# A pseudo-inverse formed in a thread of its own, and a shorter hold of the second batch

## The chip, the cores and the metric

The kernel runs on one core of one Trainium2 chip. The metric is the device time of one execution in microseconds (us), as a median of runs; profiles come from a single profiled execution.

## The reference

Landmark attention (32 landmarks) over 8 batches, 8 heads, 576 tokens and 64 columns a head, then a Fourier mix of the result and an MLP, with weights w1 (512 x 2048) and w2 (2048 x 512). Cut to what matters:

```python
# q_lm, k_lm: means of 18 tokens each, 32 landmarks
A = sm(q, k_lm); Bm = sm(q_lm, k_lm); C = sm(q_lm, k)      # row softmax of scaled products
Z = Bm.T / (norm1(Bm) * norminf(Bm) + 1e-06)
for _ in range(6):
    Z = 2 * Z - Z @ Bm @ Z
out = A @ Z @ C @ v
u = x + real(fft(fft(x, axis=1), axis=2))                  # x: the heads of out side by side
un = (u - mean) / sqrt(var + 1e-06)
result = u + relu(un @ w_ch1) @ w_ch2
```

## The kernel before

The kernel writes one long program for the five engines. `Kernel.run` is a planner: it holds generators ("threads") with priorities, and lets the first one that is due write instructions, until that one yields a time to wait. The planner's clock `self.now` is its own estimate of TensorE's time; `till(...)` is the estimated wait until tiles are ready, and `banks=` adds the wait for a free PSUM bank. The order of TensorE's instructions is exactly the order in which the threads write them, and TensorE runs them in that order: an instruction that waits holds back all behind it. The order on the other engines is arranged by the scheduler of the language.

The threads are: `attention` (priority 1), which runs `tokens` for one batch after the other; `landmarks` of a batch (priority 0), spawned from `tokens`; `weights` (priority 2), which decodes w1 and w2 from 64-bit words and splits each into a high and a low half of 16 bits, 32 pieces in all; and `mlp` (priority 3). The MLP works on chunks of 256 tokens (two tiles). For each of eight pairs of hidden blocks it forms a first product (24 matmuls `h<-unT,w`) and a second product (12 matmuls `acc<-w,h`), which trails two pairs behind. `self.seconds` counts the second products written so far. In chunk 0 the first four hidden tiles lie in buffers of the pool "mid" (seven), the others in the pool "h" (four).

Attention of a batch is two parts that meet in `mix`:
- `tokens`: sums of the landmarks (`lm`), splits of q, the products A (`at<-kbd,big`), their softmax, transposes, and the Fourier sums along the tokens (`CS`).
- `landmarks`: the product B of the landmarks and its row softmax `nrm`; C (`at<-big,qbd`, four PSUM banks) with its exponentials `Ces`; the norm product `psn` (`at<-nrm,ones_bd`), which gives the scale `ci` (and `nci`, its negative) of the inverse; the block-diagonal form `Bbd` of B, its transpose `BT`, and E = I - ci * BT'BT; the transposes `ETs` of `Ces` and their product with v, which gives R. Then comes an iteration of six steps: E is squared, and R is multiplied by I + E at each step. Both stand side by side in the tile `RE` (32 columns of E, 64 of R), so one step is `at<-RE,E` with 96 columns for each of two groups of four heads. Last, `at<-RE,Bbd` and `at<-Bbd,RE` give the small matrix from which `Wx`, `Wt` and the tables `WC` for `mix` come.

Batch 1 starts when w1 is split. In both its parts stands a hold, before C and before A:

```python
while b == 1 and self.seconds < NF // 2 - HB:   # NF // 2 - HB = 4
    yield 0.5
```

All f32 matmuls appear as two instructions each in the profile, f32 transposes as one. In the profile's names, `at` is a PSUM tile of the attention, `big`, `mid` and `row` are buffers, `h` a hidden tile, `acc` the sum of second products, `u` the normalised rows' input, `unT` its transpose by DMA. In `at<-RE,E` the tile E is stationary and RE moves.

Of the kernel before, what the change touches and what calls it, by code (L numbers as in the profile page):

```python
# [10 lines left out]
F32 = mybir.dt.float32  # L11
# [3 lines left out]
ALU = mybir.AluOpType  # L15
AX = mybir.AxisListType

P = 128
H, S, D, LM, DM, DF = 8, 576, 64, 32, 512, 2048
NF = DF // P  # L20
# [6 lines left out]
BIG, MID, ROW, UB, HB, NT, PSH = 8, 7, 6, 7, 4, 3, 2  # L27
# [6 lines left out]
MARGIN, NM, AM, M0 = 1.5, 2.0, 2.0, 0.2  # L34
# [91 lines left out]
class Kernel:  # L126
# [67 lines left out]
    def mm(self, out, a, b, start=True, stop=True, share=1.0):  # L194
        self.there[out.name] = self.now
        self.now += share * (0.42e-3 if a.dtype == F16 else 1.0e-3) * math.prod(b.shape[1:])
        self.nc.tensor.matmul(out, a, b, start=start, stop=stop, skip_group_check=True)  # L197

    def tr(self, out, a, ident):
        self.there[out.name] = self.now  # L200
        self.now += 0.11
        self.nc.tensor.transpose(out, a, ident)  # L202
# [155 lines left out]
    def tokens(self, b, st):  # L358

        nc, mm, mm3, tr, sm, split = self.nc, self.mm, self.mm3, self.tr, self.sm, self.split  # L360
        V, A = self.V, self.A
# [27 lines left out]
        e, r = yield from self.pow2(am, 4, "ab")  # L389
# [15 lines left out]
        for g in range(2):  # L405
# [5 lines left out]
                )  # L411
            if g == 0:
                yield self.till(qhs[0], kbd)
        while b == 1 and self.seconds < NF // 2 - HB:
            yield 0.5

        scr = self.small(1, "scr")
# [3 lines left out]
        for u in range(3):  # L421
            yield self.till(qhs[min(u, 1)])
            ps = self.psum()
            nh, scA = (16, sc[:, 4 + u : 5 + u]) if u < 2 else (4, scr)
            for j in range(4) if u < 2 else range(2):
                rows, at, g = (slice(0, P), 128 * j, u) if u < 2 else (slice(64 * j, 64 * j + 64), 0, j)
# [6 lines left out]
            pv, av = (t[:, 0:w].rearrange("p (h m) -> p h m", m=32) for t in (ps, ae))  # L433
# [11 lines left out]
        for u in range(3):  # L445
            ae, w = aes[u], 512 if u < 2 else 128
            AT = (self.mid() if u < 2 else self.row()).bitcast(F16)[:, 0 : 2 * w].rearrange("p (y t) -> p y t", y=2)
            if b < 2:
                yield self.till(ae, banks=1)
                ps = self.psum()  # L450
# [31 lines left out]
        for x in range(2):  # L482
            yield self.till(*Fs, banks=2)
            pss = [self.psum(), self.psum()]
            for g in range(2):
                for o in range(2):
                    i = (3, 0)[o] if x == 0 else (1, 2)[o]
# [12 lines left out]
        st["CS"] = CS  # L500
        st["tokens"] = [*st["AT"], CS]

    def landmarks(self, b, st):

        nc, mm, tr, sm = self.nc, self.mm, self.tr, self.sm
        V, A = self.V, self.A
        loads, qbd, lm = st["loads"], st["qbd"], st["lm"]
        m4g = lambda m: self.mask4.unsqueeze(1).unsqueeze(3).broadcast_to([P, 2, 4, m])
        wide = lambda src, m: src.unsqueeze(2).broadcast_to([P, 2, 4, m])
        Bd = sm.tile([P, 2, 32], F32, name="Bd")  # L510
        RE = sm.tile([P, 2, 96], F32, name="RE", bufs=3)
        Ces, crs = [], []


        ps = self.psum()
# [12 lines left out]
        nrm = sm.tile([P, 2, 2, 32], F32, name="nrm", bufs=1)  # L528
# [5 lines left out]
            rs.unsqueeze(2).broadcast_to([P, 2, 32]), ALU.mult,  # L534
        )

        while b == 1 and self.seconds < NF // 2 - HB:
            yield 0.5

        for g in range(2):  # L540
# [4 lines left out]
            for hf in range(2):  # L545
                ps = self.psum()
# [15 lines left out]
            V.reciprocal(cr, cr)  # L562
            Ces.append(Ce)
            crs.append(cr)
        yield self.till(nrm)

        psn = self.psum()
        mm(psn[:, 0:128], self.ones_bd.rearrange("p a b -> p (a b)"), nrm.rearrange("p g x m -> p (g x m)"))
        cm = self.small(4, "cm")
        V.tensor_reduce(cm, psn[:, 0:128].rearrange("p (x m) -> p x m", m=32), AX.X, ALU.max)  # L570
        ci = self.small(2, "ci")
        cmv = cm.rearrange("p (g x) -> p g x", x=2)
        V.tensor_tensor(ci, cmv[:, :, 0], cmv[:, :, 1], ALU.mult)
        V.tensor_scalar(ci, ci, 1e-6, None, ALU.add)
        V.reciprocal(ci, ci)
        nci = self.small(2, "nci")
        V.tensor_scalar(nci, ci, -1.0, None, ALU.mult)
        Bbd = sm.tile([P, 2, 4, 32], F32, name="Bbd", bufs=1)
        V.tensor_tensor(Bbd, wide(nrm[:, :, 0, :], 32), m4g(32), ALU.mult)
        yield self.till(Bbd, Ces[0])  # L580
        pst = self.psum()
        for g in range(2):
            tr(pst[:, 128 * g : 128 * g + 128], Bbd[:, g].rearrange("p a b -> p (a b)"), self.ident)
        BT = sm.tile([P, 2, P], F32, name="BT", bufs=1)
        A.copy(BT.rearrange("p g m -> p (g m)"), pst[:, 0:256])
        ETs = []
        for g in range(2):
            ET = self.mid().rearrange("p (t m) -> p t m", t=5)
            ps = self.psum()
            for t in range(4):  # L590
                tr(ps[:, 128 * t : 128 * t + 128], Ces[g][:, 128 * t : 128 * t + 128], self.ident)
            A.copy(ET[:, 0:4].rearrange("p t m -> p (t m)"), ps)
            ps = self.psum()
            tr(ps[:64, 0:128], Ces[g][:, 512:576], self.ident)
            A.copy(ET[:64, 4], ps[:64, 0:128])
            ETs.append(ET)
            if g == 0:
                yield self.till(BT, Ces[1])
                pse = self.psum()
                for i in range(2):  # L600
                    mm(pse[:, 128 * i : 128 * i + 128], BT[:, i], BT[:, i])
                E = sm.tile([P, 2, 4, 32], F32, name="E")
                for i in range(2):
                    V.scalar_tensor_tensor(
                        E[:, i].rearrange("p a b -> p (a b)"), pse[:, 128 * i : 128 * i + 128], nci[:, i : i + 1],
                        self.ident, ALU.mult, ALU.add,
                    )
                V.tensor_reduce(RE[:, :, 0:32], E.rearrange("p g a b -> p g b a"), AX.X, ALU.add)
        for g in range(2):
            yield self.till(ETs[g], loads[g][2])  # L610
            vf = loads[g][2].rearrange("p (c d) -> p c d", c=5)
            ps = self.psum()
            for t in range(5):
                n = P if t < 4 else 64
                for i in range(4):
                    mm(ps[32 * i : 32 * i + 32, 0:64], ETs[g][:n, t, 32 * i : 32 * i + 32], vf[:n, t, 64 * i : 64 * i + 64], t == 0, t == 4)
            V.tensor_scalar(RE[:, g, 32:96], ps[:, 0:64], crs[g], ci[:, g : g + 1], ALU.mult, ALU.mult)
        yield self.till(E, RE)


        for it in range(6):
            c0 = 0 if it < 5 else 32
            ps = self.psum()
            for g in range(2):
                mm(ps[:, 96 * g + c0 : 96 * g + 96], E[:, g].rearrange("p a b -> p (a b)"), RE[:, g, c0:])
            pv = ps[:, 0:192].rearrange("p (g m) -> p g m", g=2)
            nRE = sm.tile([P, 2, 96], F32, name="RE", bufs=3)
            if it < 5:
                E = sm.tile([P, 2, 4, 32], F32, name="E")
                V.tensor_tensor(E, wide(pv[:, :, 0:32], 32), m4g(32), ALU.mult)  # L630
                A.copy(nRE[:, :, 0:32], pv[:, :, 0:32])
            V.tensor_tensor(nRE[:, :, 32:96], RE[:, :, 32:96], pv[:, :, 32:96], ALU.add)
            RE = nRE
            yield self.till(E, RE, more=NM)

        ps, pst = self.psum(), self.psum()
        for g in range(2):
            mm(ps[:, 64 * g : 64 * g + 64], Bbd[:, g].rearrange("p a b -> p (a b)"), RE[:, g, 32:])
            for o in range(2):
                mm(pst[64 * o : 64 * o + 64, 64 * g : 64 * g + 64].rearrange("p (r m) -> p r m", r=2), RE[:, g, 32:], Bbd[:, g, o::2])  # L640
        wm = self.small(1, "wm")
        V.tensor_reduce(wm, ps[:, 0:128], AX.X, ALU.max, apply_absolute_value=True)
        yield self.till(wm)
# [12 lines left out]
        for i, at in enumerate((0, 32, 160, 128)):  # L656
# [3 lines left out]
            pv = ps[rows, 0:128].rearrange("p (g m o) -> p g m o", g=2, o=2)  # L660
# [5 lines left out]
        for g in range(2):  # L666
            for x in range(2):
                ps = self.psum()
# [292 lines left out]
```

## Time and profile before

| what | value |
|---|---|
| median of 3 runs | 1067.77 us (1065.95 to 1068.18) |
| the profiled execution | 1067.68 us |
| its span, first to last instruction | 1065.9 us |
| TensorE (PE) busy | 981.1 us, 92% |
| weight loads (PEld) | 681.0 us, 64% |
| VectorE (DVE) busy | 614.0 us, 58% |
| ScalarE (ACT) busy | 351.7 us, 33% |
| GpSimd (POOL) busy | 126.6 us, 12% |
| mean granted TensorE clock | 0.96 |

The page divides the span into 40 slices of 26.6 us; a digit is the busy share of a slice in tenths. A row of the table of stages gives, after the stretch, the busy time of each engine with its number of instructions in brackets, then the granted TensorE clock (1.00 is full), the DMA share and the rate. A row in order of time gives the start, the duration, the engine, the line, the operation, the output and inputs, the shape, the number of instructions merged, and in brackets how long the engine was idle before it and what ended that. A row of a group gives the number, then busy time and mean duration in ns, then the idle time before.

### The profile page before, as it was taken

Reading aid. Unit: us, or ns where it says so; the run is one execution under the profiler, and the core shown is the slowest. Engines: PE = TensorE matmul, PEld = TensorE weight load, DVE = VectorE, ACT = ScalarE, POOL = GpSimd, SP = SyncE. Lnnn points to the kernel's source line nnn. Section 1 sums busy time; section 2 is a strip of 40 time slices with the busy share of each in tenths; the row PEclk is TensorE's granted clock in tenths of the full one; section 3 lists DMA queues with packets and bytes.
Section 4 is the critical chain, followed back from the end, with each engine's and each line's share of the span. In section 5 each row is a group of like instructions: output and inputs, shape, how many; then the busy total and the mean of one; then the engine's idle time right before and its main releaser. Section 6 shows DMA issues by size and latency. Waiting matters only on the chain.

```text
span 1065.9 us, 19548 instructions
## 1 busy us (share of the span) xinstructions
PE 981.1 (92%) x8008; PEld 681.0 (64%) x8008; DVE 614.0 (58%) x1655; ACT 351.7 (33%) x791; POOL 126.6 (12%) x137
## 2 busy tenths in 40 slices
PE   1553779999999999999999999999999999999998
PEld 0442645677776677766776777667766677766665
DVE  7889888768553476446746574567451654341111
ACT  4566755324221333124322332243312332111110
POOL 0101101021101030110302030104010030110000
PEclk8556989999999999999999999999999999999999
DMA  9824402221401022111502050114111010120000
GB/s 328 311 83 129 141 25 91 70 42 39 152 21 35 26 80 103 21 31 21 179 4 50 11 164 19 40 21 129 64 41 21 21 23 20 21 50 16 5 21 20
DMA packets 85994, 71.70 MB, mean 67 GB/s; under 512 B 56336, under 2 KB 74768, under 8 KB 85776
## 3 DMA queue, kind: packets, MB, share of 16 engines
q1 hardware_dynamic: 85904, 70.45, 22.1%
q8 instruction: 63, 1.03, 0.4%
q14 instruction: 27, 0.22, 0.1%
HBM read 48.02 MB, written 9.44 MB: 54 GB/s over the span
## 4 chain that ended last, share of the span: by engine, by line
PE 86%; DVE 8%; issue 2%; ACT 2%; DMA 1%; POOL 0%; SPq 0%; ACTq 0%; DVEq 0%
PE acc L197 34%; PE h L197 34%; PE at L197 16%; DVE w L121 2%; DVE row L121 2%; DVE mid L121 1%; PE at L202 1%; ACT row L121 1%; DVE lm L121 1%; DMA big<-q_dram 0%; ACT mid L121 0%; DVE asum L121 0%; DVE u L121 0%; DVE RE L121 0%; POOL row L121 0%
## 5 line engine op out<-in xcount | busy, mean ns | idle before, releaser
L197 PE MATMUL h<-unT,w 128*128 128x256 f16 x3456 | 413.5, 274 | 20.3 <-DMA unT<-row 11.5
L197 PEld LDWEIGHTS <-w 128*128 128x128 f16 x3456 | 336.2, 98 | 92.8 <-issue 19.5
L197 PE MATMUL acc<-w,h 128*128 128x512 f16 x1680 | 394.8, 379 | 0.0
L197 PEld LDWEIGHTS <-h 128*128 128x128 f16 x1680 | 161.9, 98 | 160.5 <-issue 3.4
L121 DVE SCALAR_TENSOR_TENSOR h<-h 128x512 f16<-128x512 f32 x140 | 96.5, 689 | 247.5 <-ACT h L121 247.0
L121 ACT ACTIVATE h<-h 128x512 f16<-128x512 f32 x140 | 83.4, 596 | 367.9 <-PE h L197 367.5
L121 POOL TENSOR_TENSOR r<-ve,mhalf 128x2 f32<-128x2 f32 (+1 forms) x20 | 13.7, 683 | 446.7 <-DVE ve L121 446.7
L121 POOL TENSOR_TENSOR row<-row 128x512 f16<-128x512 f32 (+1 forms) x44 | 47.3, 1089 | 44.0 <-ACT row L121 44.0
L197 PEld LDWEIGHTS <-mid 128*128 128x128 f16 x432 | 40.2, 103 | 17.7 <-issue 9.0
L197 PEld LDWEIGHTS <-big 128*128 128x128 f16 (+1 forms) x768 | 41.3, 106 | 13.6 <-issue 2.4
L121 POOL TENSOR_TENSOR mid<-mid,asum 128x512 f32<-128x512 f32 x14 | 15.1, 1080 | 272.2 <-issue 134.5
L121 DVE TENSOR_REDUCE lm<-big 128x32 f32<-128x576 f32 (+1 forms) x48 | 44.2, 945 | 3.3 <-DMA big<-k_dram 3.2
L121 DVE SCALAR_TENSOR_TENSOR row<-at,scw,row 128x262 f32<-128x262 f32 (+1 forms) x48 | 21.4, 486 | 41.4 <-ACT row L121 27.2
L121 ACT CAST row<-row 128x512 f16<-128x512 f32 (+1 forms) x44 | 23.2, 557 | 64.5 <-DVE row L121 63.9
L121 ACT ACTIVATE row<-w 128x512 f32<-128x512 f32 x54 | 33.8, 641 | 22.8 <-DVE w L121 12.4
L197 PE MATMUL at<-RE,E 128*128 128x96 f32 (+1 forms) x192 | 31.1, 288 | 9.0 <-DVE RE L121 9.0
L121 DVE SCALAR_TENSOR_TENSOR u<-at,scw,row 128x128 f32<-128x128 f32 (+3 forms) x120 | 38.9, 389 | 0.0
L121 POOL TENSOR_TENSOR mid<-mid 128x256 f32<-128x256 f32 (+1 forms) x32 | 31.5, 987 | 61.5 <-DVE mid L121 54.0
L197 PEld LDWEIGHTS at<-RE,E 128*128 128x128 f32 x192 | 28.6, 205 | 15.3 <-issue 6.2
L121 DVE TENSOR_TENSOR mid<-mid 128x256 f32<-128x256 f32 x48 | 34.5, 743 | 1.6 <-POOL mid L121 1.4
L197 PE MATMUL at<-mid,big 128*128 128x262 f16 (+1 forms) x288 | 34.3, 293 | 0.0
L121 DVE SCALAR_TENSOR_TENSOR u<-acc,wsc,u 128x512 f32<-128x512 f32 x36 | 26.7, 745 | 11.5 <-PE acc L197 11.3
(167 smaller groups left out, 955.6 us busy)
## 6 DMA issues: line engine op xcount, KB each, us to landing
w<-w_dram SPq DMA_DIRECT2D x22, 512.0 KB, 8.9
big<-v_dram SPq DMA_DIRECT2D x16, 640.0 KB, 9.2
big<-q_dram SPq DMA_DIRECT2D x16, 584.0 KB, 5.2
big<-k_dram SPq DMA_DIRECT2D x16, 576.0 KB, 4.2
out_dram<-u SPq DMA_DIRECT2D x36, 256.0 KB, 2.0
big<-w_dram SPq DMA_DIRECT2D x10, 512.0 KB, 8.2
unT<-row SPq DMA_TRANSPOSE x72, 2.4
t<-t_dram SPq DMA_DIRECT2D x1, 1048.0 KB, 9.2
```

The costliest lines, as they stand in the source:

```text
L121: return call(out, *args, **kw)
L197: self.nc.tensor.matmul(out, a, b, start=start, stop=stop, skip_group_check=True)
L202: self.nc.tensor.transpose(out, a, ident)
```

## The change

`landmarks` now forms `psn`, `ci` and `nci` right after `nrm`, ahead of the hold and of C, and then spawns a new thread, `inverse`, with priority 0. That thread makes `Bbd`, `BT` and E, and runs the six steps without R: it carries E and the growing product of the (I + E) in a tile `EP` (32 columns each). The first step moves 32 columns, the next four 64, the last 32. Then it spreads the product to block-diagonal form (`Pbd`), multiplies it with `Bbd` and copies the result to G. `landmarks` goes on to C, the transposes and R (now a tile of its own), waits until G is there, and forms the last products from G and R. Both holds of batch 1 end after one second product, where they ended after four.

```diff
-        while b == 1 and self.seconds < NF // 2 - HB:
+        while b == 1 and self.seconds < 1:
             yield 0.5
...
+    def inverse(self, st, nrm, nci):
...
+        V.tensor_tensor(Bbd, wide(nrm[:, :, 0, :]), m4, ALU.mult)
+        yield self.till(Bbd, banks=1)
...
+            tr(ps[:, 128 * g : 128 * g + 128], flat(Bbd, g), self.ident)
...
+        A.copy(BT.rearrange("p g m -> p (g m)"), ps[:, 0:256])
+        yield self.till(BT, nci, banks=1)
...
+            mm(ps[:, 128 * g : 128 * g + 128], BT[:, g], BT[:, g])
...
+        V.tensor_reduce(EP[:, :, 0:32], E.rearrange("p g a b -> p g b a"), AX.X, ALU.add)
+        for it in range(6):
+            yield self.till(E, EP, banks=1, more=NM)
+            c0, c1 = (0 if it < 5 else 32), (64 if it > 0 else 32)
+            ps = self.psum()
+            for g in range(2):
+                mm(ps[:, 64 * g + c0 : 64 * g + c1], flat(E, g), EP[:, g, c0:c1])
...
+            if it < 5:
+                nE = sm.tile([P, 2, 4, 32], F32, name="E")
+                V.tensor_tensor(nE, wide(pv[:, :, 0:32]), m4, ALU.mult)
+                A.copy(nEP[:, :, 0:32], pv[:, :, 0:32])
+            if it == 0:
+                V.tensor_tensor(nEP[:, :, 32:64], EP[:, :, 0:32], self.diag32.unsqueeze(1).broadcast_to([P, 2, 32]), ALU.add)
+            else:
+                V.tensor_tensor(nEP[:, :, 32:64], EP[:, :, 32:64], pv[:, :, 32:64], ALU.add)
+            E, EP = nE, nEP
+        yield self.till(EP, banks=1)
+        Pbd = sm.tile([P, 2, 4, 32], F32, name="E")
+        V.tensor_tensor(Pbd, wide(EP[:, :, 32:64]), m4, ALU.mult)
+        yield self.till(Pbd, banks=1)
...
+            mm(ps[:, 128 * g : 128 * g + 128], flat(Pbd, g), flat(Bbd, g))
...
+        A.copy(G.rearrange("p g a b -> p (g a b)"), ps[:, 0:256])
+        st["G"] = G
...
     def landmarks(self, b, st):
...
+        yield self.till(nrm)
+        psn = self.psum()
+        mm(psn[:, 0:128], self.ones_bd.rearrange("p a b -> p (a b)"), nrm.rearrange("p g x m -> p (g x m)"))
...
+        self.spawn(self.inverse(st, nrm, nci))
+
+        while b == 1 and self.seconds < 1:
             yield 0.5
...
-        yield self.till(nrm)
-        psn = self.psum()
...
-            V.tensor_scalar(RE[:, g, 32:96], ps[:, 0:64], crs[g], ci[:, g : g + 1], ALU.mult, ALU.mult)
-        yield self.till(E, RE)
-        for it in range(6):
-            c0 = 0 if it < 5 else 32
...
+            V.tensor_scalar(R[:, g], ps[:, 0:64], crs[g], ci[:, g : g + 1], ALU.mult, ALU.mult)
+
+        while "G" not in st:
+            yield 0.3
+        Gt = st["G"]
+        yield self.till(Gt, R, banks=2)
...
-            mm(ps[:, 64 * g : 64 * g + 64], Bbd[:, g].rearrange("p a b -> p (a b)"), RE[:, g, 32:])
+            mm(ps[:, 64 * g : 64 * g + 64], Gt[:, g].rearrange("p a b -> p (a b)"), R[:, g])
             for o in range(2):
-                mm(pst[...], RE[:, g, 32:], Bbd[:, g, o::2])
+                mm(pst[...], R[:, g], Gt[:, g, o::2])
```

More of the change, by code (lines that the diff above doesn't have):

```diff
@@ L501, in tokens @@
         st["tokens"] = [*st["AT"], CS]
+    def inverse(self, st, nrm, nci):
+        mm, tr, sm, V, A = self.mm, self.tr, self.sm, self.V, self.A
+        m4 = self.mask4.unsqueeze(1).unsqueeze(3).broadcast_to([P, 2, 4, 32])
+        wide = lambda t: t.unsqueeze(2).broadcast_to([P, 2, 4, 32])
+        flat = lambda t, g: t[:, g].rearrange("p a b -> p (a b)")
+        Bbd = sm.tile([P, 2, 4, 32], F32, name="Bbd", bufs=1)
+        V.tensor_tensor(Bbd, wide(nrm[:, :, 0, :]), m4, ALU.mult)
[3 more added lines that the diff above has]
+            tr(ps[:, 128 * g : 128 * g + 128], flat(Bbd, g), self.ident)
+        BT = sm.tile([P, 2, P], F32, name="BT", bufs=1)
+        A.copy(BT.rearrange("p g m -> p (g m)"), ps[:, 0:256])
+        yield self.till(BT, nci, banks=1)
+        ps = self.psum()
+        for g in range(2):
+            mm(ps[:, 128 * g : 128 * g + 128], BT[:, g], BT[:, g])
+        E = sm.tile([P, 2, 4, 32], F32, name="E")
+        for g in range(2):
+            V.scalar_tensor_tensor(flat(E, g), ps[:, 128 * g : 128 * g + 128], nci[:, g : g + 1], self.ident, ALU.mult, ALU.add)
+        EP = sm.tile([P, 2, 64], F32, name="EP", bufs=3)
+        V.tensor_reduce(EP[:, :, 0:32], E.rearrange("p g a b -> p g b a"), AX.X, ALU.add)
+        for it in range(6):
+            yield self.till(E, EP, banks=1, more=NM)
+            c0, c1 = (0 if it < 5 else 32), (64 if it > 0 else 32)
+            ps = self.psum()
+            for g in range(2):
+                mm(ps[:, 64 * g + c0 : 64 * g + c1], flat(E, g), EP[:, g, c0:c1])
+            pv = ps[:, 0:128].rearrange("p (g m) -> p g m", g=2)
+            nEP = sm.tile([P, 2, 64], F32, name="EP", bufs=3)
+            if it < 5:
[11 more added lines that the diff above has]
+        yield self.till(Pbd, banks=1)
+        ps = self.psum()
+        for g in range(2):
+            mm(ps[:, 128 * g : 128 * g + 128], flat(Pbd, g), flat(Bbd, g))
+        G = sm.tile([P, 2, 4, 32], F32, name="G", bufs=1)
+        A.copy(G.rearrange("p g a b -> p (g a b)"), ps[:, 0:256])
+        st["G"] = G
@@ L507, in landmarks @@
         loads, qbd, lm = st["loads"], st["qbd"], st["lm"]
-        m4g = lambda m: self.mask4.unsqueeze(1).unsqueeze(3).broadcast_to([P, 2, 4, m])
-        wide = lambda src, m: src.unsqueeze(2).broadcast_to([P, 2, 4, m])
         Bd = sm.tile([P, 2, 32], F32, name="Bd")
-        RE = sm.tile([P, 2, 96], F32, name="RE", bufs=3)
+        R = sm.tile([P, 2, 64], F32, name="R", bufs=1)
         Ces, crs = [], []
@@ L535, in landmarks @@
         )
-        while b == 1 and self.seconds < NF // 2 - HB:
+        yield self.till(nrm)
+        psn = self.psum()
+        mm(psn[:, 0:128], self.ones_bd.rearrange("p a b -> p (a b)"), nrm.rearrange("p g x m -> p (g x m)"))
+        cm = self.small(4, "cm")
+        V.tensor_reduce(cm, psn[:, 0:128].rearrange("p (x m) -> p x m", m=32), AX.X, ALU.max)
+        ci = self.small(2, "ci")
+        cmv = cm.rearrange("p (g x) -> p g x", x=2)
+        V.tensor_tensor(ci, cmv[:, :, 0], cmv[:, :, 1], ALU.mult)
+        V.tensor_scalar(ci, ci, 1e-6, None, ALU.add)
+        V.reciprocal(ci, ci)
+        nci = self.small(2, "nci")
+        V.tensor_scalar(nci, ci, -1.0, None, ALU.mult)
+        self.spawn(self.inverse(st, nrm, nci))
+        while b == 1 and self.seconds < 1:
             yield 0.5
@@ L564, in landmarks @@
             crs.append(cr)
-        yield self.till(nrm)
-        psn = self.psum()
[L568 to L585, printed above, removed]
+        yield self.till(Ces[0])
         ETs = []
@@ L596, in landmarks @@
             ETs.append(ET)
[L597 to L608, printed above, removed]
         for g in range(2):
@@ L616, in landmarks @@
                     mm(ps[32 * i : 32 * i + 32, 0:64], ETs[g][:n, t, 32 * i : 32 * i + 32], vf[:n, t, 64 * i : 64 * i + 64], t == 0, t == 4)
-            V.tensor_scalar(RE[:, g, 32:96], ps[:, 0:64], crs[g], ci[:, g : g + 1], ALU.mult, ALU.mult)
-        yield self.till(E, RE)
-        for it in range(6):
-            c0 = 0 if it < 5 else 32
[L623 to L634, printed above, removed]
+            V.tensor_scalar(R[:, g], ps[:, 0:64], crs[g], ci[:, g : g + 1], ALU.mult, ALU.mult)
[3 more added lines that the diff above has]
+        yield self.till(Gt, R, banks=2)
         ps, pst = self.psum(), self.psum()
         for g in range(2):
-            mm(ps[:, 64 * g : 64 * g + 64], Bbd[:, g].rearrange("p a b -> p (a b)"), RE[:, g, 32:])
+            mm(ps[:, 64 * g : 64 * g + 64], Gt[:, g].rearrange("p a b -> p (a b)"), R[:, g])
             for o in range(2):
-                mm(pst[64 * o : 64 * o + 64, 64 * g : 64 * g + 64].rearrange("p (r m) -> p r m", r=2), RE[:, g, 32:], Bbd[:, g, o::2])
+                mm(pst[64 * o : 64 * o + 64, 64 * g : 64 * g + 64].rearrange("p (r m) -> p r m", r=2), R[:, g], Gt[:, g, o::2])
         wm = self.small(1, "wm")
```

## The prediction

> **What bounds the kernel now.** I read the page's slices first, then the table of stages, then the instructions of TensorE and VectorE in order of time at the two places that the change touches.
>
> ```profile
> PE   1553779999999999999999999999999999999998
> DVE  7889888768553476446746574567451654341111
> core 0: us, PE busy (x) PEld busy (x) DVE busy (x) ACT busy (x) POOL busy (x), PEclk, DMA share, GB/s
> 30.00:40.00 10.00, 7.33 (x104) 6.37 (x107) 8.09 (x28) 6.38 (x15) 0.00 (x0) 0.67 1.10 349
> 40.00:50.00 10.00, 6.10 (x81) 4.95 (x69) 9.28 (x25) 3.37 (x9) 0.89 (x2) 0.50 0.89 344
> 60.00:70.00 10.00, 6.25 (x39) 4.54 (x36) 7.12 (x18) 5.24 (x14) 0.00 (x0) 0.67 0.00 0
> 139.00:200.00 61.00, 52.77 (x430) 31.37 (x431) 50.21 (x135) 28.63 (x61) 6.94 (x8) 0.89 0.15 45
> 144.00:167.00 23.00, 18.17 (x73) 7.52 (x73) 17.00 (x49) 11.12 (x18) 0.00 (x0) 0.78 0.09 26
> 200.00:1000.00 800.00, 797.37 (x6623) 557.84 (x6621) 433.87 (x1214) 229.87 (x520) 105.19 (x110) 1.00 0.18 51
> ```
>
> From 200 to 1000 us TensorE is busy for 797.37 of 800 us at full clock. In that stage only TensorE time counts: a microsecond of work added to it is a microsecond of the result, and a wait taken away elsewhere is worth nothing. Before 200 us the kernel is bound otherwise. VectorE is busy 7 to 8 tenths and more of nearly every slice to 140 us (it decodes and splits the weights, and does batch 0's attention), and TensorE waits. From 139 to 200 us TensorE is idle for 61.00 - 52.77 = 8.2 us. So the change has two separate prices: TensorE time per batch in the saturated stage, and the order of work in the start.
>
> **Price of the products (saturated stage).** The steps of the pseudo-inverse stand between the MLP's products without a gap, so the start of one group to the start of the next is its price.
>
> ```profile
> 286.54 0.56 PE L197 MATMUL at<-RE,E 128*128 128x64 f32 x4
> 286.94 2.13 PE L197 MATMUL h<-unT,w 128*128 128x256 f16 x18
> 372.22 0.61 PE L197 MATMUL at<-BT 128*128 128x128 f32 x4
> 372.67 0.71 PE L202 MATMUL at<-ident,mid 128*128 128x128 f32 x5
> 378.37 0.58 PE L197 MATMUL at<-RE,E 128*128 128x96 f32 x4
> 378.79 2.78 PE L197 MATMUL h<-unT,w 128*128 128x256 f16 x24
> ```
>
> Four instructions (two heads' groups, two instructions for each f32 product) with 128 stationary columns take 0.40 us at 64 moving columns, 0.42 at 96, 0.45 at 128. The number of moving columns hardly matters. Before, a batch pays five steps at 96 columns and one at 64: 5 x 0.42 + 0.40 = 2.50 us. After, it pays one step at 32, four at 64 and one at 32, and the new product G at 128. No row has 32 columns; by the slope of 0.02 for 32 columns I take 0.38, and 0.40 is the upper end. That is 2 x 0.38 + 4 x 0.40 + 0.45 = 2.81 us, so +0.31 (+0.35 at the upper end). The last products keep their sizes, with G (128 columns, f32) where Bbd stood and R where RE stood. Seven batches meet a saturated TensorE (batch 1 in part), so **+2.2 us**, ends +1.9 and +2.5.
>
> The Trainium skill, "TensorE: Matmul & The Clock Gate", section "Back-to-back issue gap", prices a matmul by its moving columns, and the change would then be a gain; by its section "LDWEIGHTS (loading the stationary operand)" a load costs by its stationary columns, about 107 ns for 128, four of which make an estimated 0.43 us, and the rows above agree with this second one (0.40 to 0.45).
>
> **VectorE and ScalarE of one batch.** New are the mask product Pbd on VectorE (as the E row below, 0.42 us) and the copy of G on ScalarE (as BT, 0.37 us). Each of six additions shrinks from 128 to 64 elements (0.28 us now), which I take as nothing. After 200 us this is hidden: VectorE is busy 433.87 of 800 us there. In the start it costs 0.4 us a batch, inside the ends below. No DMA is added or moved past another; GpSimd's part is unchanged.
>
> ```profile
> L121 DVE TENSOR_TENSOR RE<-RE,at 128x128 f32<-128x128 f32 x48 | 13.4, 280 | 12.3 <-ACT RE L121 9.9 <-PE at L197 2.3
> 48.87 0.42 DVE L121 TENSOR_TENSOR E<-at,mask 128x256 f32<-128x256 f32 x1
> 31.66 0.37 ACT L121 COPY BT<-at 128x256 f32<-128x256 f32 x1 [0.72 <-PE at L202]
> L197 PE MATMUL at<-nrm,ones_bd 128*128 128x128 f32 x16 | 4.0, 332 | 4.7 <-ACT mid L121 2.9 <-DVE nrm L121 1.7
> 170.45 0.49 PE L197 MATMUL at<-nrm,ones_bd 128*128 128x128 f32 x2 [1.48 <-ACT mid L121]
> ```
>
> **The norm product ahead of C.** psn now stands behind C and needs the bank that C's exponential on ScalarE must first read: 2.9 us of TensorE waits in all, 1.48 of them in batch 1, 1.4 after it. Moved ahead of C, it doesn't have this wait. In its place the fourth of C's four banks is now psn's own, and waits for the reduction cm on VectorE; three tiles of C stand between, which hides it unless VectorE is far behind. I take **-1.0 us**, ends -1.4 and 0.
>
> **Batch 0.** Here the inverse and C part ways.
>
> ```profile
> 12.30 4.09 PE L197 MATMUL at<-big,qbd 128*64 128x288 f32 x16
> 27.69 0.37 PE L202 MATMUL at<-ident,amax 128*4 128x128 f32 x1 [11.30 <-issue]
> 29.72 0.77 PE L197 MATMUL at<-nrm,ones_bd 128*128 128x128 f32 x2 [1.66 <-DVE nrm L121]
> 46.62 1.01 PE L197 MATMUL at<-RE,E 128*128 128x96 f32 x4
> 66.82 0.69 PE L197 MATMUL at<-RE,Bbd 128*128 128x64 f32 x2 [0.38 <-DVE RE L121]
> 104.70 0.37 PE L197 MATMUL h<-unT,w 128*128 128x256 f16 x1 [11.30 <-DMA unT<-row]
> 40.99 0.34 DVE L121 TENSOR_SCALAR RE<-at,cr,ci 128x64 f32<-128x64 f32 x1 [0.23 <-PE at L197]
> 35.71 0.59 DVE L121 TENSOR_REDUCE RE<-E 128x64 f32<-128x256 f32 x1
> 13.55 0.46 DVE L121 TENSOR_REDUCE cmx<-at 128x1 f32<-128x288 f32 x1 [0.54 <-PE at L197]
> L121 DVE TENSOR_SCALAR cb<-cb 128x1 f32<-128x1 f32 x16 | 2.3, 146 | 0.0
> ```
>
> The six steps run from 46.62 to 66.82 us, some 3.4 us each, because VectorE is full. Their start E is ready at 36.3, but they wait for R (41.3) and their place in TensorE's order. In a thread of their own they could start up to 46.6 - 36.3 = 10 us earlier, and pay the two new steps Pbd and G at the end (about 2 x 2.5 us at this pace): at best 5 us earlier at the last product, so -5 is the lower end. Against this, psn waits for nrm, which is ready at 29.72, and in TensorE's order C now comes behind it: from 12.30 to about 30 us. C's four reductions (0.46 each) and ten small operations (0.146, as cb), 3.3 us in all, leave a time in which VectorE had holes and come back where it is busy 8.09 and 9.28 of 10. That is the upper end, +3.3. What follows to 140 us is limited by VectorE's sum, so an earlier last product is worth only the VectorE idle that it fills (2.9 us from 60 to 70). I take **-1 us**, nearest to the two cancelling.
>
> **Batch 1 and the hold.**
>
> ```profile
> L121 DVE SCALAR_TENSOR_TENSOR E<-at,nci,ident 128x128 f32<-128x128 f32 x16 | 5.1, 345 | 0.6 <-PE at L197 0.6
> 150.82 0.42 DVE L121 TENSOR_TENSOR Bbd<-nrm,mask 128x256 f32<-128x256 f32 x1
> 160.07 6.16 PE L197 MATMUL acc<-w,mid 128*128 128x512 f16 x20 [1.07 <-DVE w L121]
> 166.81 2.16 PE L197 MATMUL at<-big,qbd 128*64 128x288 f32 x16
> 233.02 2.75 PE L197 MATMUL acc<-w,h 128*128 128x512 f16 x12
> 162.66 0.75 DVE L121 SCALAR_TENSOR_TENSOR w<-w,wsc 128x512 f16<-128x512 f32 x1 [0.53 <-ACT w L121]
> 164.20 0.75 DVE L121 SCALAR_TENSOR_TENSOR w<-w,wsc 128x512 f16<-128x512 f32 x1 [0.79 <-ACT w L121]
> 187.63 0.74 DVE L121 SCALAR_TENSOR_TENSOR w<-w,wsc 128x512 f16<-128x512 f32 x1
> ```
>
> The hold ends when four second products stand in TensorE's order; C follows at 166.81. Up to there the second products are fed by the splits of w2, one piece every 164.20 - 162.66 = 1.54 us, and six products need a piece: 20 of them take 6.16 us where twelve later take 2.75. So from 144 to 167 us TensorE is idle for 4.8 us and on a clock of 0.78, and VectorE has 6.0 us to spare. With the hold at one product C can start some 12 us earlier, and the inverse, which does not stand behind the hold at all, from the mask product Bbd at 150.82. The lower end is all of TensorE's idle time from 139 to 200, -8.2 us. The upper end: the inverse's VectorE work (Bbd 0.42, E twice 0.345, reduction 0.59, five mask products 0.42, six additions 0.28, Pbd 0.42: 5.9 us) and C's 3.3 us come to 9.2 us where 6.0 are free, and the rest delays the w2 splits, whose last ends at 188.4: +3.2 us. I take **-4 us**, half of the idle time: VectorE can hold most of the moved work, but TensorE's order cannot fit every hole.
>
> **Sum.** The profiled execution took 1067.68 us (span 1065.9), 0.1 below the median of 1067.77. 1067.7 + 2.2 - 1.0 - 1 - 4 = 1063.9, say **1064.0 us**.
>
> **Rivals.** *No gain in the start (1067 us).* Chunk 0's first four hidden tiles lie in the seven "mid" buffers until their second products have run (the rows of acc with "mid" as operand), and batch 1's exponentials, transposes and softmax need the same buffers. Four were the condition of the old hold. Released after one, C finds buffers for its two exponentials and the rest waits for second products as before; then only the inverse's head start stays, -1 instead of -4: 1067.7 + 2.2 - 1.0 - 1 - 1 = 1066.9. For it: those buffers' count. Against it: by 166 us all four are free anyway.
>
> *Slower (1072.2 us).* C of batch 0 behind psn, which waits for the constant `diag` (issued behind the weights and landed at 25.7). If C's 3.3 us on VectorE all come on top and the release gives nothing: 1067.7 + 2.2 - 1.0 + 3.3 = 1072.2. It decides if R (41.3 now) comes later than G.
>
> ```profile
> L143 SPq DMA_DIRECT2D diag<-ny_dram x1: 1790/1790/1790, 17.7 to 17.7; - x1
> DMA to landing us min/median/max: 8.0/8.0/8.0
> ```
>
> For it: nrm at 29.72 is later than C by 17 us. Against it: TensorE had nothing else from 16.4 to 27.69, and G comes at the earliest six steps of 3.4 us after E at 36.3, so R has from 30 to some 57 us.
>
> *Narrow products are cheap (1058.6 us).* If time went with moving columns, 544 would become 32 + 4 x 64 + 32 + 128 = 448, 18% of 2.50 us saved, seven times: -3.1 instead of +2.2. The rows speak against it. This is the time that the first of the two rules of the Trainium skill named above would give.
>
> **How the numbers follow.** A measurement here tells about 0.2% (2.1 us) from no change, so faster is below 1065.6 and slower above 1069.9. The likeliest, 1064.0, has 0.43 (its own range 1057 to 1065.6), the cheap products 0.04, no gain 0.26, slower 0.27. So faster 0.47, same 0.26, slower 0.27. Ends of all terms: 1067.7 + 1.9 - 1.4 - 5 - 8.2 = 1055.0 and 1067.7 + 2.5 + 3.3 + 3.2 = 1076.7; with the outer tenths left off, 1056 to 1073.5.
>
> **What the profile after would show.** Right: the steps E at 0.38 to 0.40 us whatever their width, and a G group at 0.45; batch 1's C near 155 us, TensorE idle from 139 to 200 us cut to about 4 us, its clock from 144 to 167 near 1; batch 0's last product before 66; the psn waits behind ScalarE gone. Wrong: batch 0's C near 30 us with the first h later than 104.7; w2's last split well past 188; new TensorE waits on "mid" or cm after 200 us; or TensorE's busy time after 200 us moved by more than 3 us.

## The result, and the profile after

The change makes the kernel slower: 1091.80 us (1091.5 to 1092.27, four runs) against 1066.86 us (1065.36 to 1068.18) for the kernel before (four runs), a ratio of 1.0235 with a 95% interval of 1.0217 to 1.0252, or 25.1 us. The forecast was 1064.0 us, with an upper end of 1073.5.

The slices of the page after, TensorE and VectorE, to be set beside those of before:

```profile
PE   0653867899999999999999999999999999999998
DVE  7889788767653375535756475557552473441111
```

A tenth is too coarse to show the loss. The span grew from 1065.9 to 1090.5 us and TensorE's busy time from 981.1 to 984.1, so 3.0 of the 24.6 us are work and 21.6 are idle time. The table of stages of the kernel after says where (stretch, then busy time of TensorE, its weight loads, VectorE, ScalarE, GpSimd, then TensorE's granted clock, DMA share and rate):

```profile
139.00:167.00 28.00, 18.39 (x106) 9.88 (x106) 22.90 (x77) 14.60 (x31) 0.00 (x0) 0.88 0.11 37
167.00:200.00 33.00, 25.80 (x267) 16.22 (x268) 25.19 (x57) 14.74 (x33) 7.43 (x8) 0.90 0.29 95
200.00:1000.00 800.00, 784.86 (x6541) 549.82 (x6539) 438.11 (x1220) 230.16 (x524) 104.62 (x110) 1.00 0.18 49
```

From 139 to 200 us TensorE is idle for 9.6 + 7.2 = 16.8 us, where it was 8.2. From 200 to 1000 us it is idle for 15.1 us, where it was 800 - 797.37 = 2.6. The two make 21.1 of the 21.6 us. So the stage that I had taken as saturated, where "only TensorE time counts", lost most: 12.5 us. These are single profiles; the prices further down come from the medians of the runs.

TensorE's waits from 200 us to the end of attention name the cause there (waiting operation and tile, releaser; then total us, count, longest). First the kernel before, whose list has these two rows, then three of the nine rows of the kernel after:

```profile
PE at L197 <- ACT mid L121: 1.4, 2, 0.9
PE at L197 <- DVE mid L121: 1.1, 1, 1.1
```

```profile
PE at L202 <- ACT mid L121: 8.2, 6, 1.6
PE acc L197 <- DVE u L121: 1.7, 1, 1.7
PE at L197 <- DVE nrm L121: 0.7, 2, 0.3
```

L202 is a transpose. Its six waits stand in the six batches from 2 on, each time directly behind C. The six rows left out come to 4.4 us. The instructions of TensorE in order of time show one of them in batch 2, and the exponential on ScalarE that ends it. Before:

```profile
240.52 2.14 PE L197 MATMUL at<-big,qbd 128*64 128x288 f32 x16
242.59 0.82 PE L197 MATMUL acc<-w,h 128*128 128x512 f16 x3
243.25 1.47 PE L197 MATMUL h<-unT,w 128*128 128x256 f16 x12
244.56 0.41 PE L197 MATMUL at<-nrm,ones_bd 128*128 128x128 f32 x2
244.80 0.27 PE L202 MATMUL at<-ident,amax 128*4 128x128 f32 x1
```

After:

```profile
246.80 0.39 PE L197 MATMUL at<-nrm,ones_bd 128*128 128x128 f32 x2
247.12 2.16 PE L197 MATMUL at<-big,qbd 128*64 128x288 f32 x16
249.95 0.50 ACT L121 ACTIVATE mid<-at,cb 128x288 f32<-128x288 f32 x1 [3.64 <-DVE cb L121]
250.59 0.27 PE L202 MATMUL at<-ident,amax 128*4 128x128 f32 x1 [1.31 <-ACT mid L121]
250.70 1.46 PE L197 MATMUL acc<-w,h 128*128 128x512 f16 x6
```

C (`at<-big,qbd`) takes four banks. In the kernel before, fifteen MLP matmuls stood behind C, then psn, then the transpose of the maxima of A (`ident,amax`): here C's exponentials had read their banks by then (in two other batches psn still waited, the 1.4 us above). In the kernel after, psn stands ahead of C, the planner's wait for `amax` has run out by the time C is written, and the transpose stands directly behind C. It needs the bank that the exponential at 249.95 has yet to read, and TensorE stands for 1.31 us. The six matmuls of a second product right behind it use other banks, and the hidden tiles that VectorE had to write were finished at 247.0. The wait that psn had was not removed: it passed to the next product behind C, and became larger.

### The profile page after: what moved, and what is told of

Its sections match the earlier page's. It is cut to its first block, busy times and chain, and to the rows that moved or that the text cites. A ratio compares the mean times of both kernels' runs of the same rounds, so it can differ in the third digit from the quotient of the medians.

```text
span 1090.5 us, 19641 instructions
## 1 busy us (share of the span) xinstructions
PE 984.1 (90%) x8040; PEld 682.9 (63%) x8040; DVE 617.1 (57%) x1663; ACT 354.1 (32%) x799; POOL 127.0 (12%) x137
## 3 DMA queue, kind: packets, MB, share of 16 engines
q8 instruction: 63, 1.03, 0.4%
## 4 chain that ended last, share of the span: by engine, by line
PE 80%; DVE 11%; ACT 4%; issue 2%; POOL 1%; DMA 1%; SPq 0%; ACTq 0%; DVEq 0%; POOLq 0%
PE acc L197 33%; PE h L197 32%; PE at L197 14%; DVE w L121 2%; DVE mid L121 1%; DVE row L121 1%; ACT mid L121 1%; DVE lm L121 1%; DVE cmx L121 1%; PE at L202 1%; ACT row L121 1%; POOL row L121 1%; DVE h L121 1%; ACT big L121 1%; DMA unT<-row 1%
## 5 line engine op out<-in xcount | busy, mean ns | idle before, releaser
L121 DVE SCALAR_TENSOR_TENSOR row<-at,scw,row 128x262 f32<-128x262 f32 (+1 forms) x48 | 21.5, 486 | 42.1 <-ACT row L121 25.2
L197 PEld LDWEIGHTS at<-EP,E 128*128 128x128 f32 x192 | 29.5, 210 | 16.4 <-DVE EP L121 7.3
L197 PE MATMUL at<-EP,E 128*128 128x64 f32 (+1 forms) x192 | 30.2, 284 | 9.6 <-DVE EP L121 8.6
L121 DVE SCALAR_TENSOR_TENSOR u<-acc,wsc,u 128x512 f32<-128x512 f32 x36 | 26.6, 745 | 10.7 <-PE acc L197 10.6
```

Source lines behind the costliest of these rows:

```text
L121: return call(out, *args, **kw)
```

## Experiments

Three accounts of the loss were on trial first: the product behind C that waits for a bank, the shorter hold, and the place of batch 1's B behind twelve matmuls of the MLP. Later came the price of the thread by itself and the place of psn, batch by batch. Ratios are to the kernel before, run on the same chip, with 95% intervals; a difference of two of them carries about 0.2%, or 2 us.

**The hold alone, and the thread alone.** The kernel before with both holds at one second product:

```diff
-        while b == 1 and self.seconds < NF // 2 - HB:
+        while b == 1 and self.seconds < 1:
```

> Only the two holds of batch 1 are shortened from four second products to one; the pseudo-inverse stays as before. Theory 1 (the early release sets batch 1's VectorE and ScalarE work ahead of the w2 splits, whose last one ends some 8 us later): about 1075 us (+8), last w2 split near 196 us, no new waits after 200 us. Rival (the hold is harmless, the thread and its place in TensorE's order cost everything): 1067 us, within 2.

Measured: 1068.62 us, 1.0021 (1.0009 to 1.0034), +2.2 us. The complement, the kernel after with both holds back at `NF // 2 - HB`:

> The thread of its own as in the change, but both holds at four second products as before. Theory 1 and theory 2 together (the thread costs 3 us of TensorE time and about 8 us of waits of the amax transpose for a bank that ScalarE still reads): about 1079 us, last w2 split back near 188 us, six waits of 1.3 us at the amax transpose after 200 us. Rival (the hold costs nothing): still 1090 to 1092 us.

Measured: 1084.96 us, 1.0169 (1.0144 to 1.0194), +18 us. On the old code the short hold costs little, and the thread with its moved psn costs most. The two do not add to 25.1: with psn ahead of C, the short hold costs some 7 us.

**The bank wait behind C.** The planner is told to count the banks before it writes the `amax` transpose, which lets MLP products go first. This in the kernel after, and then in the version with the old hold:

```diff
         yield self.till(am, more=AM)
+        while self.till(banks=1) > 0.0:
+            yield self.till(banks=1)
```

> The changed kernel, and the planner holds back the amax transpose until a bank is free by its own estimate; nothing else. Theory 2: the waits of the amax transpose behind ScalarE (8.2 us after 200 us) go, 1082 to 1084 us. Rival (the waits only moved idle time that would stand elsewhere): 1090 us or more, with the same idle time under another name.

> Both together: holds at four and the amax transpose held back for a free bank. If the two causes add: about 1070 us, which is before plus the 3 us of TensorE work. Rival (a third cause in the start, batch 0's C behind the norm product): 1075 us or more, with TensorE idle before 139 us above that of before.

Measured: 1081.96 us, 1.0146 (1.0130 to 1.0163), and 1076.91 us, 1.0097 (1.0080 to 1.0115). The wait alone is worth 9.5 us with the short hold and 7.7 with the old one. TensorE's order in batch 2, in the version with the old hold, shows eighteen matmuls of first products where the wait was:

```profile
242.02 2.16 PE L197 MATMUL at<-big,qbd 128*64 128x288 f32 x16
244.11 2.14 PE L197 MATMUL h<-unT,w 128*128 128x256 f16 x18
246.09 0.27 PE L202 MATMUL at<-ident,amax 128*4 128x128 f32 x1
```

So the bank wait is shown, as a good third of the loss, and 10.3 us stay with the old hold.

**Is it batch 1's B?** In the kernel after, B of batch 1 is written behind twelve matmuls `acc<-w,mid`, which make one whole second product (where the expectations speak of twelve second products, these matmuls are meant). Here the second products of chunk 0 wait until B is written (on top of the version just shown):

```diff
+        self.begun = b
...
-            while self.split_w[1] < 2 * i + 2:
+            while self.split_w[1] < 2 * i + 2 or (ch == 0 and self.begun < 1):
```

> The thread, holds at four, amax transpose held back for a bank, and the first second product waits until batch 1's product B is written, so that B stands before it in TensorE's order as in the kernel before. Theory 3 (what is left of the cost in the start comes from B standing behind twelve second products, which wait for w2 splits): 1070 to 1072 us, TensorE idle from 139 to 200 us near 9 us. Theory 4 (it comes from the inverse's VectorE work among the w2 splits): 1075 to 1077 us, as without it.

Measured: 1076.00 us, 1.0095 (1.0079 to 1.0110). No gain: in this version B's place is not the cause. Next, batch 1's inverse also held back until four second products are written, so that its work on VectorE cannot delay the splits of w2:

```diff
+        while b == 1 and self.seconds < NF // 2 - HB:
+            yield 0.5
         Bbd = sm.tile([P, 2, 4, 32], F32, name="Bbd", bufs=1)
```

> As the kernel with B first, and batch 1's inverse starts only after four second products are written. Theory 4: 1069 to 1071 us, last w2 split near 188 us as before, and the kernel with B first is slower by 4 us or more. Theory 3: the same time as the kernel with B first, within 1 us.

Measured: 1074.58 us, 1.0081 (1.0067 to 1.0094). The last split of w2 starts at 180.68 us, 9.5 us earlier than in the version above (190.19) and 7 us earlier than in the kernel before (187.63). The time does not follow: it is 1.5 us shorter than above, and the intervals overlap. The end of the splits does not decide.

**The thread with psn left behind C.** The block that makes psn, `ci` and `nci` and spawns the thread goes behind C's loop, where it was; the holds are as before, then at one:

```diff
-        yield self.till(nrm)
-        psn = self.psum()
-        ...
-        self.spawn(self.inverse(st, nrm, nci))
         while b == 1 and self.seconds < NF // 2 - HB:
             yield 0.5
...
             crs.append(cr)
+        yield self.till(nrm)
+        psn = self.psum()
+        ...
+        self.spawn(self.inverse(st, nrm, nci))
         yield self.till(Ces[0])
```

> The thread of its own, but the norm product and the spawn stand behind C as before, holds at four. Theory 2 (the place of the norm product ahead of C makes the amax transpose wait): no waits of the amax transpose after 200 us, and about 1074 to 1077 us, that is 8 to 10 us below the thread with the norm product ahead. Rival (the thread's own products next to C make it wait): 1083 to 1085 us, with the waits still there.

> The thread behind C for all batches, with the holds at one second product. If the hold costs by itself what it cost the kernel before (0.2%): 1074 us. Rival (the hold costs 7 us wherever the thread is, as it did with the norm product ahead of C): 1079 us.

Measured: 1071.95 us, 1.0057 (1.0044 to 1.0070), and with the short hold 1071.00 us, 1.0044 (1.0030 to 1.0058). Most of the loss is gone with one move: it lies in the place of psn, alone or together with the short hold, and not in the thread. With psn behind C the short hold costs nothing that can be measured.

**What the thread itself costs, by batches.** The thread (psn behind C) for batches 2 to 7 with the old code in 0 and 1, and the reverse:

```diff
-        self.spawn(self.landmarks(b, st))
+        self.spawn(self.landmarks(b, st) if b >= 2 else self.landmarks_old(b, st))
```

> The thread behind C for batches 2 to 7 only, batches 0 and 1 as in the kernel before, holds at four. If the price of the thread where TensorE is saturated is its products alone: six batches by 0.31 us, +1.9 us, about 1067.5 us, with no new waits after 200 us. Rival (the thread costs more there, by waits or by its breaks between the MLP's products): +4 us or more.

> The other part: the thread behind C for batches 0 and 1 only, the rest as before. If the rest of the cost of the thread lies in the start (TensorE's order: B behind twelve second products, and two more steps before batch 0's last product): +3 to +5 us, about 1070 us. Rival (the start is unchanged by it): +1 us or less.

Measured: 1068.92 us, 1.0020 (1.0011 to 1.0029), +2.1 us; and 1069.87 us, 1.0038 (1.0025 to 1.0050), +4.1 us. The sum, 6.2, is the 6.1 of the version with both. The 2.1 us fit the price of the products in six batches, for which the prediction's term gives 6 x 0.31 = 1.9: TensorE's waits after 200 us come to 2.8 us there, where they were 2.5.

**Psn ahead of C, batch by batch.** From the version with psn behind C and the short hold, psn goes ahead of C in batch 0 alone, in batch 1 alone, and in batches 2 to 7:

```diff
+        ahead = b == 0        # or b == 1, or b >= 2
+        if ahead:
+            yield from scale()   # psn, ci, nci, spawn
         while b == 1 and self.seconds < 1:
...
+        if not ahead:
+            yield from scale()
```

> As the thread behind C with holds at one, but the norm product and the spawn stand ahead of C in batch 0 alone. If batch 0's C may wait for the constant without harm, since TensorE had nothing else then: within 1 us of the thread behind C for all (0.44% above before). Rival (the slower case of the prediction: C's late VectorE work lengthens the start): 3 us or more above it.

> The same with the norm product ahead of C in batch 1 alone. If what is left of the cost of its place lies in batch 1, where C now waits in TensorE's order for nrm and for the second products between: 7 to 10 us above the thread behind C for all, about 1079 us. Rival: within 2 us of it.

> The same with the norm product ahead of C from batch 2 on. If the cost there is the six waits of the amax transpose for a bank and little else: 8 to 10 us above the thread behind C for all, about 1080 us. Rival (those waits are hidden by other idle time): within 2 us of it.

Measured: 1074.12 us, 1.0067 (1.0052 to 1.0083); 1078.60 us, 1.0110 (1.0093 to 1.0128); 1082.65 us, 1.0147 (1.0132 to 1.0162). Less the 1.0044 of their base, in us:

| part | cost |
|---|---|
| thread, psn behind C, short hold | 0.44%, 4.7 us |
| psn ahead of C in batch 0 | 0.23%, 2.5 us |
| in batch 1 | 0.66%, 7.0 us |
| in batches 2 to 7 | 1.03%, 11.0 us |
| sum | 2.36%, 25.2 us |
| the change, measured | 2.35%, 25.1 us |

Each row carries some 2 us, so the agreement to 0.1 us is closer than it could be relied on to be; but nothing of the size of a row is missing. The 7.0 us of batch 1 hold for the short hold only. With both holds at four, psn's place costs 1.69% - 0.57% = 1.12%, or 12 us, in all batches, and the rows of batches 0 and 2 to 7 alone come to 13.5. So the 7 us that the short hold costs with psn ahead of C, and the 7.0 us of batch 1, are the same 7 us: by this subtraction, which carries some 3 us, the two moves cost them together and neither does alone.

TensorE's waits after 200 us in the last of the three come to 11.7 us, these rows 10.7 of them:

```profile
PE at L202 <- ACT mid L121: 8.3, 6, 1.6
PE acc L197 <- DVE u L121: 1.7, 1, 1.7
PE at L197 <- DVE nrm L121: 0.7, 2, 0.3
```

In the base the same list comes to 2.4 us, so the waits are 9.3 of the 11.0; its largest row is this one:

```profile
PE at L197 <- ACT mid L121: 1.2, 2, 0.6
```

In batch 0 the delay can be followed to the MLP. The transposes of `Bbd`, with which the inverse begins, the last product with G and the first of the MLP, in the base:

```profile
34.81 0.69 PE L202 MATMUL at<-ident,Bbd 128*128 128x128 f32 x2
67.46 0.48 PE L197 MATMUL at<-G,R 128*64 128x64 f32 x4
102.60 0.37 PE L197 MATMUL h<-unT,w 128*128 128x256 f16 x1 [12.06 <-DMA unT<-row]
```

and with psn ahead in batch 0:

```profile
37.55 0.69 PE L202 MATMUL at<-ident,Bbd 128*128 128x128 f32 x2 [1.58 <-ACT mid L121]
69.81 0.48 PE L197 MATMUL at<-G,R 128*64 128x64 f32 x4
104.96 0.37 PE L197 MATMUL h<-unT,w 128*128 128x256 f16 x1 [12.07 <-DMA unT<-row]
```

The last two moved by the same 2.4 us, and the runs by 2.5. In the twelve versions with the thread in batch 0, the distance between these two is 35.1 to 35.2 us: the MLP's start moves with the end of the landmarks. The delay is there from the inverse's beginning: behind C the transposes of `Bbd` wait 1.58 us for ScalarE and come 2.7 us later, although psn itself comes 2.2 us earlier (27.93 against 30.08).

In batch 1, the base:

```profile
151.51 0.42 PE L197 MATMUL at<-lm,qbd 128*64 128x32 f32 x8
151.77 2.14 PE L197 MATMUL at<-big,qbd 128*64 128x288 f32 x16
155.33 0.27 PE L202 MATMUL at<-ident,amax 128*4 128x128 f32 x1 [1.42 <-ACT mid L121]
156.74 0.38 PE L197 MATMUL at<-nrm,ones_bd 128*128 128x128 f32 x2
159.39 0.38 PE L197 MATMUL at<-ab_d,ones 4*128 4x4 f32 x2 [0.53 <-ACT mid L121]
166.64 0.63 PE L197 MATMUL at<-EP,E 128*128 128x32 f32 x4 [1.04 <-DVE EP L121]
```

and with psn ahead in batch 1:

```profile
151.16 0.42 PE L197 MATMUL at<-lm,qbd 128*64 128x32 f32 x8
155.62 0.49 PE L197 MATMUL at<-nrm,ones_bd 128*128 128x128 f32 x2 [1.17 <-DVE nrm L121]
156.04 2.16 PE L197 MATMUL at<-big,qbd 128*64 128x288 f32 x16
159.83 0.38 PE L197 MATMUL at<-ab_d,ones 4*128 4x4 f32 x2 [1.62 <-ACT mid L121]
164.18 0.44 PE L202 MATMUL at<-ident,Bbd 128*128 128x128 f32 x2 [1.48 <-ACT mid L121]
170.16 0.60 PE L197 MATMUL at<-EP,E 128*128 128x32 f32 x4 [0.61 <-DVE EP L121]
```

In the base C directly follows B and fills the time in which VectorE and ScalarE make `nrm`. Ahead of C, psn comes only 1.1 us earlier, and C comes 4.3 us later. TensorE now waits 1.17 us for `nrm`, and its two waits for ScalarE behind C are 1.62 and 1.48 us where they were 1.42 and 0.53. Even the first step of the inverse, for which psn was moved, starts 3.5 us later. How these delays make up the 7.0 us is not shown.

**Two tests on the kernel before.** One: its psn waits behind C (1.4 us after 200) taken away by letting the planner count the bank. Two: a longer hold.

```diff
-        yield self.till(nrm)
+        yield self.till(nrm, banks=1)
```

> The kernel before, and the planner lets the norm product wait for a free bank by its own estimate; nothing else. If the 2.9 us of waits of the norm product behind ScalarE are real time: 1063.5 to 1065 us, and no such wait in the trace. Rival (they only hide other waits): 1066 us, no change.

```diff
-        while b == 1 and self.seconds < NF // 2 - HB:
+        while b == 1 and self.seconds < 6:
```

> The kernel before with both holds at six second products. If an earlier release costs by setting batch 1's work among the w2 splits, a later one could gain: 1063 to 1066 us. Rival (batch 1 is then late, and TensorE runs out of work): 1068 us or more.

Measured: 1071.53 us, 1.0055 (1.0042 to 1.0069), and 1071.28 us, 1.0049 (1.0034 to 1.0065). The first was a miss. Where psn had waited in two batches, `amax` now stands before it, and waits 0.58 us for ScalarE in each: the bank's wait passed to another product again. The later order also made the steps of the pseudo-inverse wait for VectorE, as the largest row of its waits shows:

```profile
PE at L197 <- DVE RE L121: 5.4, 4, 1.7
```

So this test moved the bank's wait (1.2 us where it was 1.4) and paid for the new order; whether taking it away would gain stays open. With the second, holds of one, four and six give +2.2, 0 and +5.2 us on the old code. None of the versions beats the kernel before.

## Why the prediction was wrong, point by point

**What bounds the kernel.** I read the 2.6 us of idle time from 200 to 1000 us as a property of the stage. It is a property of TensorE's written order: with psn moved ahead of C from batch 2 on and nothing else changed, TensorE's busy time in these 800 us fell from 797.48 to 788.31 us.

**"Price of the products": right.** In the kernel after, groups of 64, 32 and 128 moving columns, each with the group that starts behind it:

```profile
418.61 0.55 PE L197 MATMUL at<-EP,E 128*128 128x64 f32 x4
419.00 1.46 PE L197 MATMUL acc<-w,h 128*128 128x512 f16 x6
423.56 0.53 PE L197 MATMUL at<-EP,E 128*128 128x32 f32 x4
423.93 2.11 PE L197 MATMUL acc<-w,h 128*128 128x512 f16 x9
428.49 0.61 PE L197 MATMUL at<-Bbd,E 128*128 128x128 f32 x4
428.94 2.75 PE L197 MATMUL acc<-w,h 128*128 128x512 f16 x12
```

0.39, 0.37 and 0.45 us, where 0.40, 0.38 and 0.45 were taken; six batches cost 2.1 us by the runs (1.2 to 3.1). The rival of cheap narrow products falls. Of the two rules of the Trainium skill, "TensorE: Matmul & The Clock Gate", the trace agrees with "LDWEIGHTS (loading the stationary operand)", by which the prediction estimated 0.43 us: 0.37 us at 32 moving columns and 0.45 at 128. This does not speak against its section "Back-to-back issue gap", which gives the formula that goes by moving columns for a matmul by itself, and says that it comes out too low for few columns; the prediction left that out. With the fixed 2.5 ns a matmul of that formula the rival's saving is an estimated 15.5% where the prediction took 18%, which makes 1059.0 us of its 1058.6.

**"The norm product ahead of C" (-1.0, ends -1.4 and 0): this step failed, by the most.** The waits of psn behind ScalarE went, as forecast. I asked what psn itself would wait for in its new place, and found three tiles of C to cover it. I did not ask what would now stand first behind C. From 200 us on the term is +11.0 us, and the six bank waits of the `amax` transpose are 8.3 us of idle time in it. New waits on "mid" after 200 us were among the signs of being wrong, but no term had a price for them.

**"Batch 0" (-1, ends -5 and +3.3): wrong sign, within the ends.** The steps of the kernel after:

```profile
28.43 3.54 PE L197 MATMUL at<-big,qbd 128*64 128x288 f32 x16
42.72 0.60 PE L197 MATMUL at<-EP,E 128*128 128x32 f32 x4 [0.37 <-DVE EP L121]
66.50 1.19 PE L197 MATMUL at<-Bbd,E 128*128 128x128 f32 x4 [1.43 <-DVE E L121]
68.15 0.69 PE L197 MATMUL at<-R,G 128*128 128x64 f32 x2 [0.46 <-ACT G L121]
104.93 0.37 PE L197 MATMUL h<-unT,w 128*128 128x256 f16 x1 [12.05 <-DMA unT<-row]
```

The head start was there, 42.72 against 46.62, and would have been larger with psn behind C (40.46 in the base's trace). The two added steps ate it: the last products begin at 68.15, where they began at 66.82. C came at 28.43, as forecast (about 30), and this costs 2.5 us. The slower rival had this move and nearly its size (3.3) for batch 0, but that is a tenth of the loss, and its condition, R later than G, is not met: the last products wait for G (0.46 us). An earlier end of the chain does move the MLP's first product one for one, which I had denied with "only the VectorE idle that it fills". The thread with psn behind C does start the MLP no later, and mostly earlier: its first product comes at 101.68 to 102.60 us in five profiles, with the old code in batch 0 at 102.63 to 105.38 in five, and with psn ahead of C at 104.93 to 105.74 in seven. Still it is no gain: its 4.1 us in batches 0 and 1 are measured, and come later. With the thread in batches 0 and 1 alone, TensorE is idle for 13.4 us from 139 to 200 us, where it was 8.2. Which wait there is the cause stays open.

**"Batch 1 and the hold" (-4, ends -8.2 and +3.2): wrong sign, outside the ends.** In the kernel after:

```profile
159.08 0.49 PE L197 MATMUL at<-nrm,ones_bd 128*128 128x128 f32 x2 [1.17 <-DVE nrm L121]
159.50 2.16 PE L197 MATMUL at<-big,qbd 128*64 128x288 f32 x16
189.79 1.11 PE L197 MATMUL at<-EP,E 128*128 128x64 f32 x4 [3.84 <-DVE EP L121]
```

C came 7.3 us earlier than before (near 155 had been forecast), the clock from 144 to 167 us rose from 0.78 to 0.85 (near 1 forecast), and the idle time from 139 to 200 us doubled. The longest wait there is a step of the inverse that waits 3.84 us for VectorE. I had costed the hold and left psn's place out of this term. The hold alone is +2.2 on the old code and nothing with psn behind C; psn's place in batch 1 costs nothing that can be measured while the holds are at four (by the subtraction above); together they cost 7.0 us. That w2's last split came later (195.87 against 187.63) was named as a sign of the loss, and it is one, but not its cause: with the split at 180.68 the time stayed. The rival of the "mid" buffers, with a gain of 1 instead of 4, covers no loss of this size.

**Sum.** +2.2 - 1.0 - 1 - 4 = -3.8 was forecast. By the runs it is +2.1 (products, six batches) with +4.1 (thread in batches 0 and 1), -1.5 for the short hold (within its uncertainty), and +2.5, +7.0 and +11.0 for psn's place in batch 0, in batch 1 (together with the short hold) and in the rest.

## What to carry to other kernels

When a product is moved in the order of an engine that runs in order, cost not only its own wait in the new place but also the product that takes its old place: behind a group that fills every bank of its pool, the next product from that pool waits for the first reader, unless enough work on other banks stands between. A large group whose inputs are ready early is the filler that hides the chain beside it, so a short product that must wait for that chain does not belong ahead of it. A saturated stage is saturated by its order, and an idle time near zero there does not mean that a reorder is free.

## What the runs showed of the hardware that was not expected

A product that waits for one bank stopped TensorE for 1.31 us in batch 2 with matmuls of a second product ready behind it, and six such waits took 8.2 us in the kernel after. The price of a small f32 group of four instructions went down by only 0.02 us from 64 to 32 moving columns (0.39 to 0.37).
